# A cached grouped-query attention block on one core: the output weights in longer rows, another transposition of o, and P\*V issued one batch later near the end

## The chip, the cores and the metric

The kernel runs on one core of one Trainium2 chip. The metric is the device time of one execution in microseconds (us); a lower time is better. Times quoted without a qualifier are medians of fast runs. A profile is one execution recorded by the hardware profiler. Its span is about 1.8 us shorter than the time of the same execution (2.2 us in e5): 367.5 against 369.29 us in the kernel before, 367.7 against 369.88 in e5.

Five engines matter here: PE (TensorE, matrix products), DVE (VectorE), ACT (ScalarE), POOL (GpSimd), and SP, which issues the DMA transfers. PEld is the weight load of PE. The kernel gives each engine its own list of instructions and lets it wait for the others by semaphores. In the traces of both kernels the instructions of an engine start in the order of its list: those of DVE, for one, in all 32 batches.

## The reference, cut to what matters

```python
B, Sq, D = 32, 4, 1024
Hq, Hkv, Sk, Dh = 32, 4, 2048, 128
q = (x @ wq) -> (B, Hq, Sq, Dh)
scores = q @ k^T * Dh**-0.5        # each K head serves 8 Q heads
p = softmax(scores);  o = p @ v
return o -> (B, Sq, Hq * Dh) @ wo
```

All data is bf16. K and V are 64 MiB each, 2 MiB per batch; wq and wo are 8 MiB each. So the kernel must read 144 MiB, about 151 MB. (Below, a "2 MB transfer" is one of 2 MiB.)

## The kernel before

The 32 batches go through a software pipeline. In iteration i, PE computes the scores of batch i. DVE takes their maximum, ACT the exponentials (P), DVE transposes P in 32x32 blocks (`pt`), and POOL copies the transposed P into a block-diagonal buffer (`pd`, four copies of about 1.08 us). From that buffer PE multiplies P by V (`pe_pv`, 64 small products). DVE also transposes K of the next batch (`kt`, four pieces of 1.2 us). Eight 16 KB-per-partition slots (`big`) take turns holding K, V, and at the end wo.

The parts that the argument needs:

```python
def pt(i):                                   # DVE; PT_sb has two buffers
    p.op("dve", transpose(PT_sb[i % 2] <- P_sb),
         [("exp", i)] + ([("pd", i - 2, G - 1)] if i > 1 else []), ("pt", i))

def pd(i):                                   # POOL; PD_sb is one buffer
    for g in range(G):
        p.op("pool", copy(pd_of(i)[g] <- PT_sb[i % 2]),
             [("pt", i), ("pv", i - 1)], ("pd", i, g))          # cut: start and last batches

# ... cut ...
for i in range(B):
    if i < L:
        qd(i + 1); kt(i + 1, (0, 1))         # half of the next K on DVE
    pe_qk(i)                                 # scores on PE
    softmax_max(i)                           # DVE
    if i >= 3:
        pe_ot(i - 3); ot_evac(i - 3)         # transpose of o, PE and ACT
    softmax_exp(i)                           # ACT
    # ... cut ...
    if i < L:
        kt(i + 1, (2, 3))
    pt(i)                                    # waits for exp(i) and for pd(i-2)
    if i >= 2:
        pe_pv(i - 2); o_evac(i - 2)          # P*V two batches behind the scores
    if i >= 1:
        pd(i - 1)                            # copies of P one batch behind
```

The transpose `pt(i)` reuses the buffer that `pd(i-2)` reads, and `pd(i-2)` is issued in iteration i-1, one iteration earlier. And the order on PE in one iteration is: scores(i), transpose of o, P\*V(i-2).

After the loop, `oproj` multiplies o by wo: 64 products of 512 columns, all of which need o of the last batch.

## Time and profile before

| | before |
|---|---|
| time | 369.21 us (368.9 to 369.26, 3 runs; a fourth, taken with the change, makes it 369.13 below) |
| span of the profile | 367.5 us |
| last V transfer complete (completion counts in the trace) | 340.8 us |
| last P\*V starts | 342.8 us |
| output projection | 348.7 to 364.4 us |
| last wo transfer complete | 362.2 us |

The page of the kernel before shows the span in 40 slices of 9.2 us: the clock that PE was granted in tenths, the busy share of the DMA engines in tenths, and the rate.

```profile
PEclk9997888999999999999999998998999998999989
DMA  8999999999999999999999999999999999999992
GB/s 326 437 432 428 428 430 426 428 426 425 424 426 428 424 426 428 425 428 424 428 428 426 429 426 427 424 430 424 428 426 424 428 424 430 426 428 409 386 374 86
```

The DMA engines are busy for eight tenths or more of every slice but the last, and from the fourth slice on the rate is 424 to 430 GB/s. A 2 MB transfer lands every 4.9 us, so a batch (K and V) takes 9.8 us. Only in the last slices, where wo is loaded, does the rate fall.

Next, the timeline of the kernel before, around the end of the loop and the start of the projection. The columns are start, duration, engine, line, operation, what is written and read, the count of merged instructions, and in brackets how long the engine was idle before and what released it.

```profile
320.31 4.32 POOL L314 COPY PD_sb<-PT_sb 32x1024 f32<-32x1024 f32 x4 [4.19 <-PE ps_r L321]
323.70 2.29 DVE L289 TENSOR_REDUCE mx<-ps_s 128x1 f32<-128x2048 f32 x1
...
326.22 2.58 ACT L294 ACTIVATE P_sb<-ps_s,negmx 128x2048 bf16<-128x2048 f32 x1 [1.72 <-DVE negmx L290]
...
326.25 3.73 PE L321 MATMUL ps_r<-big,PD_sb 128*128 128x128 bf16 x64 [2.53 <-DMA big<-in_v_cache_dram]
...
328.87 1.25 DVE L302 STREAM_TRANSPOSE PT_sb<-P_sb 128x1024 f32<-128x1024 f32 x1 [0.41 <-ACT P_sb L294]
...
342.84 3.75 PE L321 MATMUL ps_r<-big,PD_sb 128*128 128x128 bf16 x64
...
347.56 0.23 PE L334 MATMUL ps_r<-ident,o_sb 128*128 128x128 bf16 x1 [0.92 <-ACT o_sb L328]
...
348.69 0.41 PE L349 MATMUL ps_s<-big,QT_sb 128*128 128x512 bf16 x1 [0.90 <-ACT QT_sb L338]
```

P\*V of a batch waits 2.5 us for its V transfer: the loop runs at the pace of the DMA queue. The P-transpose waits only for the exponentials, 0.4 us. At the end, P\*V of the last batch is followed by an evacuation, a transpose, another evacuation, and the projection.

The windows view gives busy time per engine in a stretch, the granted clock, and the DMA rate. Three stretches of the kernel before:

```profile
core 0: us, PE busy (x) PEld busy (x) DVE busy (x) ACT busy (x) POOL busy (x), PEclk, DMA share, GB/s
342.00:356.00 14.00, 12.11 (x106) 6.42 (x91) 0.75 (x2) 2.39 (x5) 0.00 (x0) 0.88 1.05 386
346.00:349.40 3.40, 1.58 (x17) 0.87 (x13) 0.00 (x0) 1.55 (x3) 0.00 (x0) 1.00 1.06 389
349.40:352.80 3.40, 3.40 (x10) 0.66 (x5) 0.00 (x0) 0.00 (x0) 0.00 (x0) 0.50 1.05 386
```

While wo is loaded in 2 KB rows the rate is 386 GB/s. Before the projection PE was busy for 1.58 of 3.40 us, and in the next 3.40 us it was granted half its clock (PEclk 0.50): ten products where 16 would fit at the 0.215 us from one product to the next that the rest of the projection shows. Below, "half clock" means this, and a "window" of it is such a stretch of 3.4 us.

### The profile page before, as it was taken

How to read it: one execution, taken by the hardware profiler on the slowest of the kernel's cores; microseconds unless marked ns; L12 is line 12 of the kernel's file. 1: busy time of each engine (PE TensorE's matmuls, PEld its weight loads, DVE VectorE, ACT ScalarE, POOL GpSimd, SP SyncE). 2: the span in 40 equal slices, each digit the busy share in tenths (PEclk: the TensorE clock that was granted, in tenths of full speed). 3: DMA queues.
4: the chain of work that ended last, by engine and by line, in shares of the span. 5: the costliest groups of instructions: out<-in, count | busy, mean ns of one | idle time of the engine just before them, and what ended most of it. 6: DMA issues, size and time to landing. Idle time of an engine off the chain costs nothing.

```text
span 367.5 us, 5961 instructions
## 1 busy us (share of the span) xinstructions
PE 276.3 (75%) x2744; PEld 142.7 (39%) x2272; DVE 275.6 (75%) x273; ACT 123.4 (34%) x135; POOL 164.2 (45%) x262
## 2 busy tenths in 40 slices
PE   1872458888777777888887777878777777778796
PEld 1001003444444444444444443535334445445722
DVE  0029687999999999999998988797998888784300
ACT  1020211444444444333344334242344433455200
POOL 5001150555555555555544455555555443448100
PEclk9997888999999999999999998998999998999989
DMA  8999999999999999999999999999999999999992
GB/s 326 437 432 428 428 430 426 428 426 425 424 426 428 424 426 428 425 428 424 428 428 426 429 426 427 424 430 424 428 426 424 428 424 430 426 428 409 386 374 86
DMA packets 14506, 151.90 MB, mean 413 GB/s; under 512 B 1296, under 2 KB 1552, under 8 KB 5776
## 3 DMA queue, kind: packets, MB, share of 16 engines
q1 hardware_dynamic: 14336, 151.39, 97.8%
q8 instruction: 20, 0.33, 0.4%
q10 hardware_dynamic: 144, 0.13, 0.1%
q14 instruction: 6, 0.05, 0.0%
HBM read 151.26 MB, written 0.26 MB: 412 GB/s over the span
## 4 chain that ended last, share of the span: by engine, by line
DMA 43%; PE 28%; DVE 15%; ACT 7%; issue 6%; SPq 1%
DMA big<-in_v_cache_dram 38%; PE ps_s L16 14%; DVE mx L289 10%; ACT P_sb L294 6%; DMA big<-in_wq_dram 6%; PE ps_r L321 6%; PE ps_s L281 5%; PE ps_s L349 2%; DVE KT_sb L269 2%; DVE PD_sb L314 1%; DVE QT_sb L242 1%; DVE negmx L290 1%; DVE KT_sb L226 1%; SPq L156 0%; ACT QT_sb L338 0%
## 5 line engine op out<-in xcount | busy, mean ns | idle before, releaser
L314 POOL COPY PD_sb<-PT_sb 32x1024 f32<-32x1024 f32 x121 | 125.6, 1038 | 135.4 <-DVE KT_sb L269 59.5
L269 DVE STREAM_TRANSPOSE KT_sb<-big 128x1024 f32<-128x1024 f32 x128 | 150.8, 1217 | 8.1 <-DMA big<-in_k_cache_dram 8.0
L321 PE MATMUL ps_r<-big,PD_sb 128*128 128x128 bf16 x1984 | 120.3, 223 | 33.4 <-DMA big<-in_v_cache_dram 31.3
L321 PEld LDWEIGHTS ps_r<-big,PD_sb 128*128 128x128 bf16 x1984 | 116.1, 100 | 40.9 <-POOL QD_sb L260 32.5
L294 ACT ACTIVATE P_sb<-ps_s,negmx 128x2048 bf16<-128x2048 f32 x32 | 81.8, 2556 | 81.2 <-DVE negmx L290 81.2
L16 PE MATMUL ps_s<-KT_sb,QD_sb 128*128 128x512 bf16 x384 | 106.7, 386 | 0.0
L289 DVE TENSOR_REDUCE mx<-ps_s 128x1 f32<-128x2048 f32 x32 | 73.3, 2292 | 18.3 <-PE ps_s L16 17.7
L281 PE MATMUL ps_s<-KT_sb,QD_sb 128*128 128x512 bf16 x128 | 49.7, 388 | 41.0 <-ACT P_sb L294 34.7
L338 ACT ACTIVATE QT_sb<-ps_r 128x128 bf16<-128x128 bf16 x32 | 23.6, 736 | 104.2 <-PE ps_r L334 104.2
L281 PEld LDWEIGHTS ps_s<-KT_sb,QD_sb 128*128 128x128 bf16 x128 | 12.5, 98 | 118.1 <-issue 72.4
L302 DVE STREAM_TRANSPOSE PT_sb<-P_sb 128x1024 f32<-128x1024 f32 x32 | 39.9, 1246 | 14.7 <-ACT P_sb L294 14.7
L260 POOL COPY QD_sb<-QT_sb 32x64 f32<-32x64 f32 x128 | 29.4, 230 | 40.7 <-DVE QT_sb L242 25.5
L328 ACT ACTIVATE o_sb<-ps_r,rinv 128x128 bf16<-128x128 f32 x32 | 11.8, 370 | 16.1 <-PE ps_r L321 16.0
L357 DVE CAST y_sb<-ps_s 128x512 bf16<-128x512 f32 x1 | 0.7, 691 | 21.4 <-PE ps_s L349 21.4
L226 DVE CAST KT_sb<-ps_r 128x512 bf16<-128x512 f32 x2 | 1.3, 686 | 20.0 <-PE ps_r L210 20.0
L349 PE MATMUL ps_s<-big,QT_sb 128*128 128x512 bf16 x32 | 13.2, 412 | 0.9 <-ACT QT_sb L338 0.9
L16 PE MATMUL ps_s<-big,QT_sb 128*128 128x512 bf16 x32 | 13.1, 411 | 0.0
L334 PEld LDWEIGHTS ps_r<-ident,o_sb 128*128 128x128 bf16 x32 | 3.1, 96 | 23.4 <-issue 21.6
L349 PEld LDWEIGHTS ps_s<-big,QT_sb 128*128 128x128 bf16 x32 | 4.7, 147 | 11.4 <-issue 11.2
L228 ACT ACTIVATE KT_sb<-ps_r 128x512 bf16<-128x512 f32 x2 | 1.1, 595 | 23.6 <-PE ps_r L16 23.6
L16 PE MATMUL ps_s<-big,P_sb 128*128 128x512 bf16 x32 | 8.8, 400 | 0.0
L210 PEld LDWEIGHTS ps_r<-big,P_sb 128*128 128x128 bf16 x8 | 0.8, 98 | 19.7 <-issue 11.3
(30 smaller groups left out, 68.3 us busy)
## 6 DMA issues: line engine op xcount, KB each, us to landing
big<-in_k_cache_dram SPq DMA_DIRECT2D x32, 2048.0 KB, 29.2
big<-in_v_cache_dram SPq DMA_DIRECT2D x32, 2048.0 KB, 33.0
big<-in_wq_dram SPq DMA_DIRECT2D x4, 2048.0 KB, 14.0
big<-in_wo_dram SPq DMA_DIRECT2D x7, 1024.0 KB, 19.1
big<-in_wo_dram SPq DMA_DIRECT2D x1, 512.0 KB, 12.7
big<-in_wo_dram SPq DMA_DIRECT2D x2, 256.0 KB, 10.2
P_sb<-in_x_dram SPq DMA_DIRECT2D x1, 256.0 KB, 2.8
out_dram<-y_sb SPq DMA_DIRECT2D x1, 128.0 KB, 1.8
```

The costliest lines, as they stand in the source:

```text
L16: return eng.add_instruction(mybir.InstMatmult(name=nc.get_next_instruction_name(), engine=eng.engine, start_tensor_calc=start, stop_tenso ...
L260: p.op("pool", lambda e, s=src, d=dst: e.tensor_copy(d, s), waits if g == 0 else [], ("qd", i) if g == G - 1 else None)
L269: p.op("dve", lambda e, s=src, d=dst: e.transpose(d, s), waits, ("kt", i, c))
L281: mm = lambda e, a_=(out_, lhsT, rhs), f=first, l=last: e.matmul(a_[0], lhsT=a_[1], rhs=a_[2], start=f, stop=l, skip_group_check=True)
L289: p.op("dve", lambda e: e.tensor_reduce(mx[:, i % 4:i % 4 + 1], ps_s[:, :], AX.X, ALU.max), [("qk", i)], ("mx", i))
L294: p.op("act", lambda e: e.activation(P_sb[:, :, :, :].rearrange("p t r w -> p t w r"), ps_s[:, :].rearrange("p (t w r) -> p t w r", w=2, r=R),
L302: p.op("dve", lambda e: e.transpose(dst, src), [("exp", i)] + ([("pd", i - 2, G - 1)] if i > 1 else []), ("pt", i))
L314: p.op("dve" if i == B - 1 and g < 3 else "pool", lambda e, s=src, d=dst: e.tensor_copy(d, s), waits, ("pd", i, g))
L321: p.op("pe", lambda e, t=t: e.matmul(buf[:, 0:Dh], lhsT=pd_of(i)[:, t // 2, :, :, t % 2].rearrange("p g q -> p (g q)"), rhs=big[:, slot_of ...
L328: p.op("act", lambda e: e.activation(o_sb[:, :], buf[:, 0:Dh], ACT.Copy, scale=rinv[:, i % 4:i % 4 + 1]), [("pv", i), ("rinv", i)] + ([("o ...
L338: p.op("act", lambda e: e.activation(oT_sb[:, i * Sq:(i + 1) * Sq, :].rearrange("p s h -> p h s"), buf[:, 0:128].rearrange("p (h s) -> p h ...
L349: mm = lambda e, a=(out_, lhsT, rhs), h=h: e.matmul(a[0], lhsT=a[1], rhs=a[2], start=(h == 0), stop=(h == Hq - 1), skip_group_check=True)
```

## The change

Its intent: load wo faster, at the end where nothing else hides it; and let the scores run ahead of the V transfers near the end, so that PE does not wait for V before it can start the next scores. For this the last K is loaded before V(27), and from batch 24 on P\*V runs three batches behind the scores. A third P buffer (`PF_sb`, in a slot of `big` that is free by then) takes the copies of batches 28 and 31.

The diff, cut to its core:

```diff
+    SW = 24
-        oT_sb = QT_sb[...]                       # o transposed shared the queries' space
+        oT_sb = sbuf("oT_sb", [128, Hq // 2, 2, NT], BF16)
+        a, b = loads.index(("v", B - 5)), loads.index(("k", B - 1))
+        loads[a], loads[b] = loads[b], loads[a]
+        wo_v = wo.rearrange("(h p e) n -> p h (e n)", p=128, e=2)     # 4 KB rows
 ...
         def pd_of(i):
-            return PE_sb if i == B - 2 else PD_sb
+            return PE_sb if i == B - 2 else PF_sb if i in (B - 4, B - 1) else PD_sb
 ...                                             # pd: all four copies of the last batch on POOL
         def pe_ot(i):
-            p.op("pe", transpose(buf[:, 0:128] <- o_sb, ident), ...)
+            for e_ in range(2):
+                for u in range(2):               # even/odd columns x half identity
+                    p.op("pe", matmul(buf[64*u:64*(u+1), 64*e_:64*(e_+1)], lhsT, rhs), ...)
 ...
         for i in range(B):
+            j = i - 2 if i < SW else i - 3 if i > SW else -1
 ...
             pt(i)
-            if i >= 2:
-                pe_pv(i - 2)
-                o_evac(i - 2)
-            if i >= 1:
-                pd(i - 1)
+            if j >= 0:
+                pe_pv(j)
+                o_evac(j)
+            if i == L - 2:
+                zero(PF_sb, [("pv", B - 6)], "pf0")
+            if 0 < i != SW:
+                pd(i - 1 if i < SW else i - 2)
```

## The prediction

> **What bounds it now.** Up to about 341 us, the DMA queue: the rate row holds 424 to 430 GB/s; a 2 MB transfer lands every 4.9 us, 9.8 us per batch. Between 66 and 170 us the chain of waits has the scores loop at 8.9 us per batch, inside that. After 341 us compute ends it. In the timeline the last V has landed by about 341, its P\*V starts at 342.84, o is transposed at 347.56, and the output projection runs without a pause from 348.69 to 364.2: 64 products of 0.215 us, plus about 1.7 us because the windows view gives clock 0.50 from 349.4 to 352.8. wo, moved at 387 GB/s against 424 before (windows view), has landed by about 362, ahead of its use. Tail: evacuation and store, 3.3 us.
>
> **What the change does.**
> 1. wo in 4 KB runs: between the 2 KB and 16 KB rates I estimate 408 GB/s; wo lands about 1 us sooner, off the critical path.
> 2. Four products for one transpose (0.22 us): I estimate 0.25 to 0.4 us together, partly repaid by a simpler evacuation (now 0.74). About zero.
> 3. K(31) lands 4.9 us sooner, which helps only if the scores can use it.
> 4. From batch 24, P\*V three behind. The catch: in iteration i the P-transpose on DVE still waits for the copies of P(i-2), issued one iteration earlier in the kernel before. Now they are issued in the same iteration and wait for P\*V(i-3) to free the one P buffer, and that P\*V stands on PE behind scores(i). From the end of scores(i): P\*V 3.75, copies 4.3, so the P-transpose starts 8.2 us later, against 5.2 when only exp holds it; then DVE still has two K-transposes (2.4) and the maximum (2.3). Replaying the program order with the trace's durations, I estimate 10.4 us per batch instead of 9.8, from batch 25 to 29. Scores of batch 31 end about 335.5 instead of 333.5, and PE idles up to 3.7 us in every second iteration. [...] (0.50 at 349.4, after a window with a 2 us gap). So more half-clock windows, each up to 1.7 us, now on the path.
> 5. The last P copies all on POOL: 4.3 us instead of 2.9; four P\*V follow the last scores instead of three.
>
> The replay gives the old kernel within 1 us; in the new one the projection starts about 352 instead of 348.7. DMA stays saturated.
>
> **Predicted: 372 us, 368.5 to 376 (8 in 10). Faster by over 2%: 0.01; within 2%: 0.95; slower by over 2%: 0.04.**
>
> **What would show it.** Right: wo landing about 361 but the projection starting at 351 to 354 and never waiting for wo; DVE waiting on POOL's P copies before the P-transpose in batches 25 to 29, 2 to 4 us each; the chain of waits through POOL copies and P\*V there, not V transfers. Wrong: no such wait, the projection starting before 348.5, then waiting for wo: 366 to 368 us.
>
> **What would make it wrong.** A better phase than my replay has (P buffer freed earlier); a warm projection (gain 1.7); four products costing over 0.4 us each time.

## The result, and the profile after

| | before | after |
|---|---|---|
| time | 369.13 us (368.9 to 369.26, 4 runs) | 379.11 us (378.14 to 379.89, 4 runs) |
| span of the profile | 367.5 us | 376.3 us |
| output projection | 348.7 to 364.4 us | 359.3 to 373.2 us |
| last wo transfer complete | 362.2 us | 361.3 us |

The ratio of after to before is 1.027 (95% interval 1.0244 to 1.0296). Here and below a ratio is the mean time of one kernel's fast runs over that of the other's fast runs of the same rounds, so it is not quite the ratio of the quoted medians. The change is slower by 2.7%; I had predicted 372 us, 0.8% slower.

The page after, the rows that answer to those of before:

```profile
PEclk9997888999999999999999899899898796999999
DMA  8999999999999999999999999999999999999910
GB/s 334 427 434 421 437 427 421 437 420 429 428 423 428 427 428 422 430 427 427 428 425 427 429 422 427 427 427 427 434 420 430 428 423 432 425 415 409 387 49 28
```

The DMA row is as full as before until wo has landed, and then the queue is idle for the last 15 us or so. The transfers are not what became slower. The clock row dips in both kernels, but from about 268 us on more often than before: half-clock stretches start at 268.6, 289.1, 313.0 and 336.9 us here, at 305.0 and 349.4 us there.

The timeline after, over two batches (297 to 321 us) of the lagged part of the loop, and the start of the projection:

```profile
297.19 3.75 PE L331 MATMUL ps_r<-big,PD_sb 128*128 128x128 bf16 x64
...
301.06 4.32 POOL L324 COPY PD_sb<-PT_sb 32x1024 f32<-32x1024 f32 x4 [8.68 <-PE ps_r L331]
...
305.49 1.25 DVE L312 STREAM_TRANSPOSE PT_sb<-P_sb 128x1024 f32<-128x1024 f32 x1 [3.62 <-POOL PD_sb L324]
...
306.70 2.35 DVE L279 STREAM_TRANSPOSE KT_sb<-big 128x1024 f32<-128x1024 f32 x2
308.97 2.25 DVE L299 TENSOR_REDUCE mx<-ps_s 128x1 f32<-128x2048 f32 x1
...
311.44 2.52 ACT L304 ACTIVATE P_sb<-ps_s,negmx 128x2048 bf16<-128x2048 f32 x1 [4.95 <-DVE negmx L300]
...
314.16 0.58 PE L291 MATMUL ps_s<-KT_sb,QD_sb 128*128 128x512 bf16 x1 [4.30 <-ACT P_sb L304]
...
319.23 0.63 PE L291 MATMUL ps_s<-KT_sb,QD_sb 128*128 128x512 bf16 x1
...
320.67 3.75 PE L331 MATMUL ps_r<-big,PD_sb 128*128 128x128 bf16 x64
...
359.25 0.38 PE L364 MATMUL ps_s<-big,oT_sb 128*128 128x512 bf16 x1 [0.46 <-ACT oT_sb L354]
```

Read it as a circle. P\*V (297.19) releases the copies of P on POOL (301.06). These release the P-transpose on DVE (305.49), for which DVE has stood idle for 3.62 us. Behind the P-transpose in DVE's list come half of the next K-transposes and the maximum of the scores. The maximum releases the exponentials (311.44), these the scores of the next batch (314.16), and behind them in PE's list comes the next P\*V (320.67). One turn of the circle is 23.5 us and covers two batches (the turn before it took 23.1 us). Before, two batches took 19.6 us, the pace of the DMA queue.

The waits of the P-transpose between 262 us and the end of the loop, in the view of one source line, first before (line 302):

```profile
L302 DVE STREAM_TRANSPOSE PT_sb<-P_sb x8: 1245/1246/1247, 269.4 to 338.6; 128x1024 f32<-128x1024 f32 x8
its engine sat idle before it (us, times) until:
  ACT P_sb L294: 5.5, 8
```

and after (line 312):

```profile
L312 DVE STREAM_TRANSPOSE PT_sb<-P_sb x8: 1245/1245/1246, 268.6 to 347.8; 128x1024 f32<-128x1024 f32 x8
its engine sat idle before it (us, times) until:
  POOL PD_sb L324: 12.3, 5
  ACT P_sb L304: 3.4, 3
```

Five of eight P-transposes now wait for POOL, 12.3 us together. They alternate: 3.62 us before the transposes of batches 25, 27 and 29, 0.7 us before those of 26 and 28. None of these waits for POOL existed before.

And the windows view after:

```profile
289.10:295.90 6.80, 4.83 (x12) 0.54 (x4) 5.06 (x6) 2.09 (x3) 2.97 (x6) 0.50 1.01 431
302.40:325.80 23.40, 17.72 (x168) 8.30 (x144) 16.45 (x16) 6.15 (x9) 10.04 (x17) 0.85 1.01 428
313.00:319.80 6.80, 5.64 (x14) 0.54 (x4) 4.25 (x5) 1.27 (x3) 2.16 (x6) 0.50 1.00 424
...
342.00:356.00 14.00, 14.00 (x244) 13.26 (x242) 3.74 (x4) 4.11 (x8) 7.41 (x8) 1.00 1.03 407
```

Twice PE has half its clock for 6.8 us at a stretch, and both times its products are the scores, which stand on the circle. The last line shows wo at 407 GB/s with 4 KB rows, against 386.

### The profile page after: what moved, and what is told of

Same layout as the page of the kernel before. It is cut to its first block, busy times and chain, and to the rows that moved or that the text cites. A ratio compares the mean times of both kernels' runs of the same rounds, so it can differ in the third digit from the quotient of the medians.

```text
span 376.3 us, 6121 instructions
## 1 busy us (share of the span) xinstructions
PE 289.0 (77%) x2840; PEld 141.9 (38%) x2368; DVE 271.7 (72%) x270; ACT 111.3 (30%) x136; POOL 167.1 (44%) x265
## 4 chain that ended last, share of the span: by engine, by line
PE 38%; DMA 23%; DVE 20%; ACT 13%; POOL 3%; issue 2%; SPq 1%; POOLq 0%; DVEq 0%
PE ps_s L16 19%; DMA big<-in_v_cache_dram 18%; ACT P_sb L304 12%; DVE mx L299 12%; PE ps_r L331 9%; PE ps_s L291 7%; DMA big<-in_wq_dram 5%; DVE KT_sb L279 4%; POOL PD_sb L324 3%; PE ps_s L364 2%; DVE PT_sb L312 1%; DVE negmx L300 1%; DVE QT_sb L252 1%; DVE KT_sb L236 1%; PE ps_r L349 0%
## 5 line engine op out<-in xcount | busy, mean ns | idle before, releaser
L324 POOL COPY PD_sb<-PT_sb 32x1024 f32<-32x1024 f32 x116 | 120.0, 1035 | 137.7 <-PE ps_r L331 108.8
L331 PE MATMUL ps_r<-big,PD_sb 128*128 128x128 bf16 x1856 | 111.8, 222 | 10.7 <-DMA big<-in_v_cache_dram 8.8
L16 PE MATMUL ps_s<-KT_sb,QD_sb 128*128 128x512 bf16 x384 | 113.8, 406 | 0.0
L331 PEld LDWEIGHTS ps_r<-big,PD_sb 128*128 128x128 bf16 x1856 | 107.1, 100 | 13.1 <-POOL QD_sb L270 9.5
L291 PE MATMUL ps_s<-KT_sb,QD_sb 128*128 128x512 bf16 x128 | 52.5, 410 | 61.8 <-ACT P_sb L304 54.6
L354 ACT ACTIVATE oT_sb<-ps_r 128x128 bf16<-128x128 f32 x32 | 8.9, 278 | 112.2 <-PE ps_r L349 112.2
L349 PEld LDWEIGHTS ps_r<-ident,o_sb 128*64 128x64 bf16 x128 | 4.6, 109 | 30.7 <-issue 29.5
L364 PE MATMUL ps_s<-big,oT_sb 128*128 128x512 bf16 x32 | 12.1, 379 | 0.5 <-ACT oT_sb L354 0.5
L16 PE MATMUL ps_s<-big,oT_sb 128*128 128x512 bf16 x32 | 12.1, 379 | 0.0
L324 POOL COPY big<-PT_sb 32x1024 f32<-32x1024 f32 x8 | 8.3, 1036 | 4.1 <-DVE rinv L313 3.6
L349 PE MATMUL ps_r<-ident,o_sb 128*64 128x64 bf16 x128 | 8.1, 207 | 0.6 <-ACT o_sb L338 0.6
```

What stands on the lines that cost most here:

```text
L16: return eng.add_instruction(mybir.InstMatmult(name=nc.get_next_instruction_name(), engine=eng.engine, start_tensor_calc=start, stop_tenso ...
L291: mm = lambda e, a_=(out_, lhsT, rhs), f=first, l=last: e.matmul(a_[0], lhsT=a_[1], rhs=a_[2], start=f, stop=l, skip_group_check=True)
L324: p.op("pool", lambda e, s=src, d=dst: e.tensor_copy(d, s), [("pt", i), free.get(i, ("pv", i - 1))], ("pd", i, g))
L331: p.op("pe", lambda e, t=t: e.matmul(buf[:, 0:Dh], lhsT=pd_of(i)[:, t // 2, :, :, t % 2].rearrange("p g q -> p (g q)"), rhs=big[:, slot_of ...
L349: p.op("pe", lambda e, a=(out_, lhsT, rhs): e.matmul(a[0], lhsT=a[1], rhs=a[2], start=True, stop=True), waits + [("o", i)] if e_ == u == 0 ...
L364: mm = lambda e, a=(out_, lhsT, rhs), h=h: e.matmul(a[0], lhsT=a[1], rhs=a[2], start=(h == 0), stop=(h == Hq - 1), skip_group_check=True)
```

## The experiments

Theory A has two parts. First, the new lag makes `pt(i)` wait for copies issued in its own iteration, which wait for a P\*V that stands on PE behind scores(i). Second, that wait leaves PE idle long enough to lose half its clock, and the slowed scores are on the path. The rivals: (B) the work added to every batch (four products for one, zeroings, all copies on POOL) costs the time; (C) the lag or the changed order of the loads costs by itself.

All kernels below gave correct results. The kernel before was rerun beside each group. In these reruns it scattered more, from 368.4 to 372.2 us, than in the first measurement. The groups ran on different chips (e1 to e4; e5 to e7; e8 to e10), so across groups the ratios to the kernel before compare better than the times.

The third buffer for the transposed P takes the space of queries that are used up by then, and the idle-time products write into the buffer of `ring` that PE itself writes next.

### e1: only the first half of the change

```diff
 # the kernel before, plus: wo in 4 KB rows, four products for the transpose of o, oT_sb of its own
 # not changed: P*V two batches behind, order of the loads, P buffers
```

> The kernel before with only the first half of the change: wo by 4 KB rows, o transposed by four products, oT in its own buffer; P*V stays two batches behind, V(27) before K(31). Theory A (the new waits of the lagged part cost everything): within 0.3% of before, 368 to 369.5 us, perhaps 0.5 us less by the shorter evacuation of o (0.28 us instead of 0.74). Rival B (the added work in each batch costs): most of the 10 us is here, 374 us or more.

Measured: 367.82 us, ratio 0.9941 (0.9898 to 0.9983). Rival B is out for its larger part: the four products cost nothing that can be seen. They take 0.25 us together, and the evacuation after them 0.28 us instead of 0.74. The whole loss lies in the other half of the change.

### e2: the same waits, but PE kept busy in its long gaps

```diff
+        def pe_fill(n):                          # into the PSUM bank that PE itself writes next
+            buf, waits = ring[len(freed) % 4], [freed[len(freed) - 4]]
+            for _ in range(n):
+                p.op("pe", matmul(buf, lhsT=ident, rhs=<512 columns of the queries>), waits, None)
             if j >= 0:
                 pe_pv(j)
                 o_evac(j)
+            pe_fill(20 if i == SW else 16 if i in (26, 28, 30) else 0)
```

> The changed kernel with idle-time products on TensorE into an unused PSUM bank in the four long gaps (20 after the scores of batch 24, 16 after P*V in iterations 26, 28, 30; 0.216 us each, less than the gaps of 5.3 and 4.3 us). The order and the waits are the same. If the half clock is what my replay lacked (theory A, second part): no half-clock windows at 268, 289 to 296, 313 to 320 and 337 us, scores after each long gap 3.7 us instead of 5.9, two batches in about 20.7 us instead of 23.1, time 371 to 374 us. If the clock does not matter: 379 us as the change, or more.

Measured: 371.04 us, ratio 1.0023 (0.9983 to 1.0064). Adding work to PE made the kernel 8.1 us faster than the change, because the work fills idle time and keeps the clock. The windows view of e2, two batches each:

```profile
278.40:299.10 20.70, 18.36 (x184) 9.65 (x161) 16.33 (x16) 6.22 (x9) 10.08 (x17) 1.00 1.01 428
...
299.10:319.80 20.70, 18.36 (x183) 9.65 (x161) 16.33 (x16) 6.22 (x9) 10.07 (x17) 1.00 1.00 425
```

The clock is 1.00 throughout, and two batches take 20.7 us. The P-transpose still waits 12.3 us for POOL, five times, as in the change. So the two parts of theory A are separated: with the wait alone the kernel is within the scatter of before, and the half clock that follows the wait makes nearly all of the 10 us. The projection starts at 352.2 us in e2; the prediction's replay (its program order played through with the durations of the trace) had said 352.

### e3: the wait taken away

```diff
+        PT_bufs = [PT_sb[:, 0], PT_sb[:, 1], <the queries of batches 0 to 15, used up by then>]
+        def pt_of(i):
+            return i % 2 if i < SW else (0, 2, 1)[(i - SW) % 3]
 # pt(i) then waits for the copies of the last batch that used the same buffer: P(i-3)
```

> The changed kernel with a third buffer for the transposed P from batch 25 on (in the queries of batches 0 to 15, which are used up by then), so that the P-transpose of batch i waits for the copies of P(i-3), issued one iteration earlier, and no longer for those of P(i-2). All added work, the zeroings and P*V three behind stay. Theory A: no wait of DVE for POOL, 9.8 us per batch or less, projection starting at 347 to 349 us, time 366.5 to 369.5 us, so no slower than before. Rival B (added work) or rival C (V order and P*V lag by themselves): stays above 375 us.

Measured: 367.43 us, ratio 0.9923 (0.9884 to 0.9963). The waits of the P-transpose in e3 (line 325), same stretch:

```profile
L325 DVE STREAM_TRANSPOSE PT_sb<-P_sb x5: 1245/1246/1246, 270.1 to 327.9; 128x1024 f32<-128x1024 f32 x5
L325 DVE STREAM_TRANSPOSE QT_sb<-P_sb x3: 1245/1245/1246, 280.4 to 336.9; 128x1024 f32<-128x1024 f32 x3
its engine sat idle before it (us, times) until:
  ACT P_sb L304: 5.3, 8
```

No wait for POOL is left, and the projection starts at 348.6 us. All the rest of the change is in this kernel: the lag, the load order, the zeroings, all copies on POOL. So rivals B and C are out. e3 is not free of the half clock: its scores of batches 25 and 30 took 4.84 and 5.08 us, where 3.47 is usual. But its projection starts no later than that of e1 (349.1 us), whose scores took 3.47 in each batch from 23 on. So where the circle is open, these 3.0 us are hidden.

### e4 and e6: a smaller dose, without and with warm gaps

```diff
-    SW = 24
+    SW = 28
 # e6 also: pe_fill(20 if i == SW else 16 if i in (30,) else 0)
```

> The changed kernel with the lag from batch 28 on instead of 24, one number changed. Theory A: two pairs of the lagged iterations fewer, each pair costing 23.1 - 19.6 = 3.5 us, so 379 less some 7 to 9 us: 369 to 372 us. Rival B: unchanged, 378 to 380 us.

Measured: 373.48 us, ratio 1.0069 (1.0013 to 1.0124). The direction is right, the size misses: I expected 372 at most. Its scores of batches 29 and 31 took 5.13 and 5.88 us instead of 3.47, so two half-clock stretches had remained (309.7 to 313.2 and 330.2 to 337 us in its trace).

> The kernel with the lag from batch 28 on (it took 373.5 us, 1.5 us more than I expected at most) with idle-time products in its two long gaps, after the scores of batch 28 and after P*V in iteration 30. If half-clock windows (309.7 to 313.2 and 330.2 to 337 us in its trace) make the rest of its loss: 367.5 to 369.5 us. If what remains is the waits: 372 us or more.

Measured: 369.59 us, ratio 0.9962 (0.9918 to 1.0006), just above the range I gave. With the two gaps filled 3.9 us come back, or 1.07% by the ratios. The two slow blocks of scores in e4 are together 4.07 us too long (5.13 + 5.88 - 2 x 3.47), so the account closes, as far as two groups on two chips can be compared.

### e5: P\*V ahead of the scores

```diff
+            if i > SW:
+                pe_pv(j)                         # batch i-3, before the scores of batch i
             pe_qk(i)
 ...
-        loads[a], loads[b] = loads[b], loads[a]  # V(27) before K(31) again
```

> The changed kernel with the P*V of batch i-3 issued on TensorE before the scores of batch i instead of behind them, and V(27) loaded before K(31) again (else V(27) would hold the scores up); buffers, lag and added work as in the change. Theory A (that P*V stood behind the scores, so the copies of P(i-2) came too late for the P-transpose of batch i): the wait of DVE for POOL's copies falls from 3.6 us to under 1 us, about 9.8 us per batch, time 368 to 370.5 us. If instead the lag itself or the single P buffer were to blame, whatever the order on TensorE: 374 us or more.

Measured: 369.88 us, ratio 0.9982 (0.9932 to 1.0031). The waits of the P-transpose in e5:

```profile
L310 DVE STREAM_TRANSPOSE PT_sb<-P_sb x8: 1245/1246/1246, 270.3 to 339.7; 128x1024 f32<-128x1024 f32 x8
its engine sat idle before it (us, times) until:
  ACT P_sb L302: 5.5, 8
```

With the same buffers and the same lag, the wait is gone too. It came from the place of P\*V in PE's list, behind the scores, together with the reused buffer; breaking either link is enough. This run changes two things at once (order on PE and order of the loads), so it does not say what the load order alone would do.

### e7: the kernel before with a warm start of the projection

```diff
         o_evac(L)
+        pe_fill(3)
         pe_ot(L)
         ot_evac(L)
+        pe_fill(3)
```

> The kernel before with three idle-time products before and three after the last transpose of o, so that the 2 us gap ahead of the output projection is filled. If the gap is what halves the clock at the start of the projection: no half-clock window there, projection 13.9 us instead of 15.5, time 367.3 to 367.9 us, which would make the 1.5 to 2.5 us by which e1 and e3 beat the kernel before nothing of their own. Else unchanged, 369.2 us.

Measured: 368.43 us, ratio 0.9929 (0.9892 to 0.9966). The windows view of e7:

```profile
346.00:349.40 3.40, 2.81 (x20) 1.25 (x17) 0.00 (x0) 1.56 (x3) 0.00 (x0) 1.00 1.05 386
349.40:352.80 3.40, 3.40 (x18) 1.11 (x9) 0.00 (x0) 0.00 (x0) 0.00 (x0) 1.00 1.05 388
```

The clock stays at 1.00, 18 products are done where before ten were, but the time is half a microsecond above what I expected. The timeline shows why: the projection catches up with wo, which is still in 2 KB rows.

```profile
359.65 0.44 PE L355 MATMUL ps_s<-big,QT_sb 128*128 128x512 bf16 x1 [0.51 <-DMA big<-in_wo_dram]
```

PE waits 0.5 us for wo in this trace. From this I argue, and have not tested by itself, that the faster wo load is worth under a microsecond here, and only in a kernel whose projection starts early and at full clock. It also means that the lead of e1 and e3 over the kernel before is partly the half clock at the start of its projection, which their profiles do not have (in e3 the clock is 1.00 from 348.5 to 362.5 us).

### e8 and e9: the change again, and one gap of four filled

```diff
 # e8: the changed kernel as it is
 # e9: pe_fill(16 if i == 28 else 0)
```

> The changed kernel itself once more, on the chip that also runs the two below, so that the size of the half-clock part is read between kernels of one chip: 378 to 380 us, ratio 1.02 to 1.03.

Measured: 379.96 us, ratio 1.0242 (1.0198 to 1.0285), as expected.

> The changed kernel with 16 idle-time products in one of its four long gaps only, after P*V in iteration 28. If each long gap costs its own half-clock window (theory A): the window at 313 to 320 us is gone, the others stay, and 2.2 to 2.5 us of the 8 us come back, so 376 to 377.5 us. If the idle products help in some other way, or one long warm stretch is needed: 378 us or more, or all 8 us back.

Measured: 378.58 us, ratio 1.0208 (1.0166 to 1.0251). This misses: 1.4 us came back between the medians, not 2.2 to 2.5, and the runs of the two overlap. The following table shows where the rest went. It gives, worked out from the starts of the products in each trace, how long the 16 score products of a batch took. In the loop at full clock they take 3.47 us.

| scores of batch | 25 | 27 | 29 | 31 | too long in sum | time of this execution |
|---|---|---|---|---|---|---|
| change | 5.07 | 5.84 | 6.24 | 4.76 | 8.0 us | 378.14 |
| e8, change again | 5.44 | 6.04 | 6.35 | 4.82 | 8.8 us | 379.58 |
| e9, gap in iteration 28 filled | 6.07 | 6.36 | 3.47 | 6.38 | 8.4 us | 378.94 |
| e2, four gaps filled | 3.47 | 3.47 | 3.47 | 3.47 | 0 | 370.83 |

(The batches between them took 3.47 us in all four.) In e9 the filled gap did save its own batch, 29, fully. But batch 31 met two half-clock windows in place of one. In every row, the time less the sum is between 370.1 and 370.8 us. That is the strongest evidence for the size: the half clock costs 8 to 9 us, and everything else in the change together at most 2 us, which is within the scatter of the kernel before.

Where the windows fall can be read from the clock records that the traces keep. In each of the twelve traces, the starts of all half-clock stretches lie whole multiples of 3.413 us apart (in the change, after 66 us: 207.19, 237.91, 268.63, 289.11, 313.00 and 336.89 us). I cut each trace, from 66 us on, into windows on this grid and took PE's busy time in each, as the windows view counts it. Of the windows at full clock, 38 had PE busy for under 1.4 us, and every one was followed by half clock; 944 had over 1.6 us, and none was; of the 23 between, 9 were. A window at half clock was followed by another one in 9 cases, with PE busy for 2.53 us at most, and by full clock in 43, with 2.67 us at least. So the length of a gap alone does not decide. In the kernel before, two gaps of 2.53 us show it: the one from 302.80 us leaves PE 1.22 us of work in its window (301.58 to 304.99), and half clock follows; the one from 323.72 us lies across the edge of two windows, the first of which has 1.66 us of work, and none follows. The grid lies differently from trace to trace (an edge 1.2 us after the start of the span in the kernel before, 2.4 us in the change), and the same gap cost different amounts: the scores of batch 25 took 5.07, 5.44 and 6.07 us in the change, e8 and e9.

### e10: a candidate to beat both

```diff
 # e3, plus: pe_fill(20 if i == SW else 5 if i in (25, 26, 27, 28, 29) else 0)
```

> The kernel of e3 (third buffer for the transposed P) with idle-time products in the gaps of batches 24 to 29 (20 after the scores of batch 24, five after each P*V), as a candidate to beat both kernels. In e3 one half-clock window (317.4 to 320.8 us) fell on the scores of batch 30. Without it the scores of batch 31 end about 330.4 us instead of 331.5, and the projection would start about 347.6, after which wo (landed at 361.3) bounds it: 366.5 to 367.3 us against 367.4 of e3.

Measured: 368.61 us, ratio 0.9933 (0.9897 to 0.9968), not better than e3. In its trace a gap of 2.8 us before the scores of batch 30 was left, and a half-clock window (320.0 to 323.4 us) followed it. The best kernel is e3 with 367.43 us; it is 0.8% faster than the kernel before beside it, though the scatter of that kernel (369.17 to 371.88 us in that group) is of the same size. I do not know what that scatter comes from: only one execution of the kernel before was traced. The record gives a hint and no more: of its 25 reruns, 15 of the 16 that took over 370.8 us had a mean granted clock of 0.954 or less, and 8 of the 9 faster ones 0.957 or more. One half-clock window more lowers the mean over 368 us by 0.0046.

## Why the prediction was right or wrong

- **What bounds the kernel before: right.** DMA to 341 us, then compute. e7 confirms the account of the projection: filling the gap removed the half clock.
- **wo in 4 KB rows: right.** Estimated 408 GB/s and wo at 361 us; measured 407 GB/s and 361.3 us, and the projection never waited for it.
- **Four products and the evacuation: right.** Estimated 0.25 to 0.4 us; measured 0.25 us, and 0.46 us saved in the evacuation. e1 is not slower than before.
- **The new wait of the P-transpose: right in mechanism and in size.** Estimated 10.4 us per batch; e2, the same waits at full clock, shows 20.7 us for two. The wait was predicted as "2 to 4 us each" in batches 25 to 29; it alternates between 3.6 and 0.7 us, so in two of the five batches it is shorter than that. In e3, where only this wait is gone, the whole loss is gone.
- **The step that failed: "So more half-clock windows, each up to 1.7 us, now on the path."** The windows came, but this term was mis-sized, and hardly in the sum. The prediction's start of the projection at 352 us, with 13.8 us of products, 3.3 us of tail and about 1.8 us between span and time, makes 371 us; so the 372 us held about 1 us for the clock, and even that may have stood for the projection, whose half clock the prediction kept (it lists a warm projection as a gain of 1.7) and which ran at full clock in the change. In the loop the term measured 8.0 us in the change and 8.8 us in its repetition. The pieces were in the prediction: a gap "in every second iteration" (of 3.7 us; 4.3 measured, and 5.3 after batch 24), half clock after it, "on the path". What failed is that the windows were not counted and added. Four gaps at 1.7 us each already make 6.8 us, some 378 us in all, beyond the range given. The one thing that was not foreseen is that two gaps drew two windows in a row, 6.8 us: a block of scores then took up to 6.2 us instead of 3.5, a loss of up to 2.8 us for one gap and not 1.7.
- **"Within 2%: 0.95": wrong with it.** The direction was stated, but the range ended at 376 us.

After 66 us each half-clock stretch in these traces is 3.4 or 6.8 us long (those that the end of a trace cuts short apart), its start lies on the grid of 3.413 us described at e9, and from the change to its repetition and to e9 the same gaps cost different amounts. That the gaps of the new loop would bring half clock was my assumption, with one stretch of the trace before beside it (0.50 at 349.4 us). The window before that stretch was not idle: PE was busy in it for 1.6 of 3.4 us.

## What to carry to other kernels

When a consumer is moved one stage later, look for the buffer whose reuse it was already releasing in time: here a double buffer that had been freed one iteration ahead was now freed by work issued in the same iteration, and three engines, each working through its list in order, closed into a circle. Then ask where the idle time lands: here idle stretches of PE just before products on the critical path cost twice, once as the wait and once as the half clock after it, and the second was the larger (8.0 us in the change, against at most 2 us for everything else). Both can be told apart cheaply by filling the gap with products that nobody reads, and by giving the reused buffer one more copy. And if such a stretch recurs, count the half-clock windows it can draw and add them to the prediction.

## The clock and the transfers: what the runs show

- Gaps of PE of 0.9 to 2.3 us were enough for half clock in an unlucky place: half clock from 349.4 us in the kernel before, after a stretch of 3.4 us with two gaps of 0.9 us and PE busy for 1.58 us (removed by filling them, e7); and from 317.4 us in e3, at the end of a gap of 2.3 us. Another gap of 2.5 us in the loop of the kernel before (from 323.72 us), and one of 3.05 us in e6 (before the scores of batch 30), were not followed by a half clock. What separates the cases in these traces is PE's busy time in a window of the 3.413 us grid: all 38 full-clock windows with under 1.4 us were followed by half clock, none of the 944 with over 1.6 us was (see e9).
- Idle-time products into a free PSUM bank inside the kernel kept the clock at 1.00 in e2 (278.4 to 319.8 us) and took 8.1 us off the change.
- Loads by the length of a row: 386 GB/s with 2 KB rows and 407 with 4 KB, in transfers of the same sizes (1 MB and less); 424 to 430 with 16 KB, but in transfers of 2 MB, so that this last step differs in more than the row.
